# A gated MLP behind a softmax convolution on one core: the transposes one step later, the exponentials two steps earlier, and the carried tokens loaded in eight pieces

## The chip, the core and the metric

The kernel runs on one NeuronCore of a Trainium2 chip. TensorE (PE, with its weight loads shown apart as PEld) multiplies, VectorE (DVE), ScalarE (ACT) and GpSimd (POOL) work on the elements, and SyncE (SP) issues every DMA. The metric is the device time of one execution in microseconds (us). Before the change it is 1408.44 us, the median of three runs from 1408.35 to 1408.87 us.

## What is computed

The reference has two stages. The first is a causal convolution over seven tokens whose weights are a softmax of the input `weight_gen`, one set for each token and head. The second is a gated MLP with 192 inputs, 1536 hidden columns and 192 outputs over all 16384 tokens.

```
w   = exp(weight_gen - max);  w = w / (sum(w) + 1e-9)        # 8 heads, 7 taps
xa[s, h, :] = sum over k of w[s, h, k] * x_pad[s + k, h, :]  # 6 zero rows ahead of each batch
g   = xa @ w_gate                                            # [16384, 1536]
out = (g * sigmoid(g) * (xa @ w_val)) @ w_out                # [16384, 192]
```

The weights of the MLP come as 64-bit floats; the convolution's inputs are 32-bit.

## The kernel before

**Tiles.** Each of the 128 partitions holds 128 consecutive tokens, and a batch of 4096 tokens fills 32 partitions. The work goes over 32 *groups* of 4 tokens per partition, that is 512 tokens each. A group has 12 *steps*, one for each block of 128 hidden columns, so there are 384 steps, and step `i` is block `f = i % 12` of group `g = i // 12`.

**One step on TensorE.** `up_first` (L439, L442) and `up_second` (L451) multiply the transposed activations by the step's columns of both weight matrices, in three products of rounded and remainder parts each, into two PSUM buffers. ACT makes `sg`, the silu of the first buffer (L459); DVE makes `h`, the product with the second buffer (L473), and with that both buffers are read; ACT rounds it to `hi` (L474) and DVE takes the remainder `lo` (L476). Two to three steps later (`LAG = 2`) `down` (L503, L512; L496 in group 0) multiplies `hi` and `lo` by the output weights. The pool `ps_up` has four buffers, so a step's two are asked for again two steps later.

**Getting the next group ready.** During group `g - 1`, DVE makes the convolution of group `g`: seven products (L230) and their sums into `xatt` (L260), spread over nine steps. The last sum is followed by a copy on ACT (L263) that fills the second half of `xatt`. Then PE transposes `xatt` in two halves (`turn`, L299) into two more buffers of `ps_up` (tile `tr`), and ACT and DVE split the result into `xhi` (L317) and `xlo` (L324). In the step that transposes, the transposes stand on PE's queue right behind `up_first`, and the downs that a step normally has between `up_first` and `up_second` come after `up_second`. With `s0 = 12 (g - 1) - 3` (for group 1 it is -1), the sums are spread over the steps from `s0` to `s0 + 8`, and the table `turned` puts the transposes into step `s0 + 9`; that is block `f = 6` of the group before, with the last sum in block `f = 5`.

**The softmax.** The taps come in six chunks. For a chunk, DVE takes maxima and differences (L169, L176), ACT one exponential over the whole chunk (L182, 128x1344), DVE sums, reciprocals and products (L187 to L199). The exponential needs another function table than silu: ACT loads a table ahead of it and another behind it, ahead of the next silu. The table `exps` says in which step it is recorded, between `up_first` and the step's silu. Chunk 1 is recorded in step 16 (`EXP1`), and chunks 2 to 5 in steps 66, 138, 210 and 282, each time block `f = 6`.

**The head.** Ahead of step 0, SP issues the first taps, the first `x` (L141), the *carried tokens* and then the raw MLP weights (L348). The carried tokens are the last six of the partition before, which the convolution of a partition's first tokens needs; each batch's first partition has zeros instead (L149). `load_x` fetches them in four loads of 31 partitions (L150). DVE and POOL then make group 0's convolution and turn the 64-bit weights into 32-bit ones (`weight_ops`, L362 to L402), block by block, four raw blocks ahead. In group 0 DVE does all of a step's other work ahead of the step's `h` (here written as `hi`, L468).

The order on every engine is the order in which the code records the work. `spread` gives each small operation a step; within a step, the first goes between `h` and `lo`, the others behind.

Of the kernel before, what the change touches and what calls it, by code (L numbers as in the profile page):

```python
# [18 lines left out]
def dynconv_glu_kernel(  # L19
# [23 lines left out]
    nc = tc.nc  # L43
# [4 lines left out]
    P = 128  # L48
    T = B * S // P
    PAD = K - 1  # L50
# [4 lines left out]
    NF = F // P  # L55
# [4 lines left out]
    EXP1 = 16  # L60
# [34 lines left out]
    xr = x.rearrange("b (q t) d -> (b q) t d", t=T)  # L95
# [24 lines left out]
    def load_taps(c):  # L120

        j0, n = wcuts[c]
        wt = w_t[c] = soft.tile([P, NJ, H, K], F32, tag="wt", name="wt")
        pieces = {0: (0, JG, n), 1: range(0, n + 1, 2 * JG)}.get(c, (0, n))

        def load(a, b):
            nc.sync.dma_start(
                out=wt[:, a:b].rearrange("p t h k -> p t (h k)"), in_=wgr[:, j0 + a : j0 + b]
            )

        return [lambda a=a, b=b: load(a, b) for a, b in zip(pieces, pieces[1:])]

    def load_x(c):

        j0, n = xcuts[c]
        xt = x_t[c] = xin.tile([P, PAD + NX, D], F32, tag="xt", name="xt")
        pieces = {0: (0, JG, n), 1: range(0, n + 1, 2)}.get(c, (0, n))

        def load(a, b):
            own = PAD if c and a == 0 else 0  # L140
            nc.sync.dma_start(  # L141
                out=xt[:, PAD + a - own : PAD + b], in_=xr[:, j0 + a - own : j0 + b]
            )
            if c == 0 and a == 0:


                per = S // T
                for p0 in range(0, P, per):
                    nc.gpsimd.memset(xt[p0 : p0 + 1, 0:PAD], 0.0)  # L149
                    nc.sync.dma_start(  # L150
                        out=xt[p0 + 1 : p0 + per, 0:PAD],
                        in_=xr[p0 : p0 + per - 1, T - PAD : T],
                    )

        return [lambda a=a, b=b: load(a, b) for a, b in zip(pieces, pieces[1:])]

# [387 lines left out]
    turned = {}  # L544

    def spread(ops, first, last):

        for n, op in enumerate(ops):
            at = first + (n * (last - first)) // len(ops)
            todo.setdefault(max(at, 0), []).append(op)  # L550

    with tc.manual_schedule():
# [44 lines left out]
        for c in range(1, len(wcuts)):  # L597
            s0 = (wcuts[c - 1][0] // JG - 1) * NF - LEAD if c > 1 else NF
            s1 = (wcuts[c][0] // JG - 1) * NF - LEAD
            before, exponentials, after = softmax_ops(c)  # L600
            at = s0 + (s1 - s0) * 5 // 8 if c > 1 else EXP1
            if c + 1 < len(wcuts):
                todo.setdefault(s1, []).append(lambda c=c: load_taps(c + 1)[0]())
            spread(before, s0 + 1 - (c == 1), at)
            exps[at] = exponentials
            spread(after, at + 2, s1)
        for g in range(1, NG):
            s0 = (g - 1) * NF - (LEAD if g > 1 else LEAD1)
            c = first_x.get(g)
            if c and c + 1 < len(xcuts):  # L610
                todo.setdefault(s0, []).append(lambda c=c: load_x(c + 1)[0]())
            asides, rest, _ = attention_ops(g)
            spread(asides, max(s0, 0), s0 + NF - 4)
            spread(rest, max(s0, 0), s0 + NF - 3)
            turned[s0 + NF - 3] = g

        steps = [(g, f) for g in range(NG) for f in range(NF)]
        for i in range(len(steps) + LAG + 1):
            ops = todo.pop(i, [])
            to_turn = turned.get(i)  # L620
            if i < len(steps):
                g, f = steps[i]
# [75 lines left out]
```

## Time and profile before

| | before |
|---|---|
| median of the runs | 1408.44 us |
| the profiled execution | 1409.2 us, of which 1407.4 us are the span from the first to the last instruction |
| PE busy | 1300.9 us, 92% of the span |
| DVE, ACT, POOL busy | 1010.4 us, 610.2 us, 71.8 us |
| granted TensorE clock, mean | 0.988 |
| chain that ended last, by engine | PE 83%, DVE 8%, ACT 4%, DMA 2% |

The profile is of one execution. A bracket behind a row of the timeline says how long the engine sat idle before the instruction and which event ended that; the chain of waits is followed back from the last instruction. A `q` behind an engine's name means its sequencer.

### The profile page before, as it was taken

Reading aid. Unit: us, or ns where it says so; the run is one execution under the profiler, and the core shown is the slowest. Engines: PE = TensorE matmul, PEld = TensorE weight load, DVE = VectorE, ACT = ScalarE, POOL = GpSimd, SP = SyncE. Lnnn points to the kernel's source line nnn. Section 1 sums busy time; section 2 is a strip of 40 time slices with the busy share of each in tenths; the row PEclk is TensorE's granted clock in tenths of the full one; section 3 lists DMA queues with packets and bytes.
Section 4 is the critical chain, followed back from the end, with each engine's and each line's share of the span. In section 5 each row is a group of like instructions: output and inputs, shape, how many; then the busy total and the mean of one; then the engine's idle time right before and its main releaser. Section 6 shows DMA issues by size and latency. Waiting matters only on the chain.

```text
span 1407.4 us, 31625 instructions
## 1 busy us (share of the span) xinstructions
PE 1300.9 (92%) x13560; PEld 1220.4 (87%) x13560; DVE 1010.4 (72%) x1385; ACT 610.2 (43%) x1073; POOL 71.8 (5%) x66
## 2 busy tenths in 40 slices
PE   0479999999999999999999999999999999999998
PEld 0359899989999998999999899989989899999998
DVE  2997867768777777877777777777777776677743
ACT  1445444454444445444344544444454444444443
POOL 3673000000000000000000000000000000000000
PEclk9989999999999999999999999999999999999999
DMA  3341010101001010100101001010100101000000
GB/s 96 97 156 32 13 41 13 52 13 51 13 21 52 13 52 12 51 13 21 52 13 52 13 22 43 18 51 13 52 13 13 41 13 52 13 13 13 13 13 13
DMA packets 28460, 47.36 MB, mean 34 GB/s; under 512 B 1956, under 2 KB 25508, under 8 KB 26528
## 3 DMA queue, kind: packets, MB, share of 16 engines
q1 hardware_dynamic: 28320, 45.34, 9.7%
q8 instruction: 106, 1.74, 0.5%
q14 instruction: 34, 0.28, 0.1%
HBM read 32.75 MB, written 12.58 MB: 32 GB/s over the span
## 4 chain that ended last, share of the span: by engine, by line
PE 83%; DVE 8%; ACT 4%; DMA 2%; issue 1%; SPq 0%; ACTq 0%; DVEq 0%
PE dn L503 22%; PE up L451 19%; PE up L439 18%; PE up L442 17%; PE dn L512 6%; DVE xatt L260 3%; DVE h L473 2%; DMA xt<-in_x_dram 2%; ACT sg L459 2%; PE tr L299 1%; ACT xatt L263 1%; DVE m L389 1%; DVE w L402 1%; DVE m L379 0%; PE dn L496 0%
## 5 line engine op out<-in xcount | busy, mean ns | idle before, releaser
L503 PE MATMUL dn<-wo,hi 64*128 64x384 f32 x2976 | 612.7, 347 | 0.4 <-ACT hi L474 0.4
L512 PE MATMUL dn<-wo,lo 64*128 64x192 f32 x2976 | 543.0, 249 | 0.3 <-DVE lo L476 0.3
L503 PEld LDWEIGHTS dn<-wo,hi 64*128 64x128 f32 x2976 | 480.0, 185 | 14.9 <-ACT hi L474 0.6
L473 DVE TENSOR_TENSOR h<-up,sg 128x512 f32<-128x512 f32 x372 | 257.1, 691 | 289.5 <-ACT sg L459 289.4
L512 PEld LDWEIGHTS dn<-wo,lo 64*128 64x128 f32 x2976 | 444.8, 187 | 9.6 <-DVE lo L476 0.5
L459 ACT ACTIVATE sg<-up 128x512 f32<-128x512 f32 x384 | 229.7, 598 | 435.7 <-PE up L451 405.0
L474 ACT ACTIVATE hi<-h 128x512 fp32r<-128x512 f32 x372 | 235.2, 632 | 294.7 <-DVE h L473 294.7
L476 DVE TENSOR_TENSOR lo<-h,hi 128x512 fp32r<-128x512 f32 x372 | 255.8, 688 | 70.5 <-ACT hi L474 70.5
L439 PE MATMUL up<-xhi,wb_hi 64*128 64x512 f32 x768 | 246.8, 425 | 10.8 <-ACT sg L459 7.5
L451 PE MATMUL up<-xhi,wa_hi 64*128 64x512 f32 x768 | 240.4, 427 | 9.8 <-POOLq L280 9.7
L439 PE MATMUL up<-xlo,wb_hi 64*128 64x512 f32 x768 | 234.0, 395 | 0.9 <-DVE xlo L324 0.9
L439 PE MATMUL up<-xhi,wb_lo 64*128 64x512 f32 x768 | 234.0, 396 | 0.0
L442 PE MATMUL up<-xhi,wa_lo 64*128 64x512 f32 x768 | 233.0, 393 | 0.0
L442 PE MATMUL up<-xhi,wa_hi 64*128 64x512 f32 x768 | 233.0, 393 | 0.0
L442 PE MATMUL up<-xlo,wa_hi 64*128 64x512 f32 x768 | 231.8, 390 | 0.0
L451 PE MATMUL up<-xhi,wa_lo 64*128 64x512 f32 x768 | 226.1, 392 | 0.0
L451 PE MATMUL up<-xlo,wa_hi 64*128 64x512 f32 x768 | 225.6, 391 | 0.0
L230 DVE TENSOR_TENSOR prod<-xt,wt 128x768 f32<-128x768 f32 x186 | 182.0, 979 | 0.1
L260 DVE TENSOR_TENSOR xatt<-xatt,prod 128x768 f32<-128x768 f32 x186 | 180.7, 971 | 0.0
L439 PEld LDWEIGHTS up<-xhi,wb_hi 64*128 64x128 f32 x768 | 138.3, 186 | 16.4 <-ACT sg L459 8.3
L442 PEld LDWEIGHTS up<-xlo,wa_hi 64*128 64x128 f32 x768 | 138.9, 187 | 8.1
L442 PEld LDWEIGHTS up<-xhi,wa_lo 64*128 64x128 f32 x768 | 138.1, 185 | 8.8
(57 smaller groups left out, 1370.3 us busy)
## 6 DMA issues: line engine op xcount, KB each, us to landing
xt<-in_x_dram SPq DMA_DIRECT2D x14, 1344.0 KB, 5.6
out_dram<-osb SPq DMA_DIRECT2D x31, 384.0 KB, 2.6
raw<-in_moe_w_out_dram SPq DMA_DIRECT2D x12, 192.0 KB, 2.7
wt<-in_weight_gen_dram SPq DMA_DIRECT2D x3, 672.0 KB, 3.9
raw<-in_moe_w_gate_dram SPq DMA_DIRECT2D x12, 128.0 KB, 2.6
raw<-in_moe_w_val_dram SPq DMA_DIRECT2D x12, 128.0 KB, 2.6
wt<-in_weight_gen_dram SPq DMA_DIRECT2D x4, 224.0 KB, 3.7
xt<-in_x_dram SPq DMA_DIRECT2D x2, 384.0 KB, 3.7
```

Of the source, the lines that this page charges most:

```text
L230: engine.tensor_tensor(out=into.rearrange("p t (h i) -> p t h i", h=H), in0=src, in1=w, op=ALU.mult)
L260: nc.vector.tensor_tensor(out=a, in0=a, in1=tmp.pop(k), op=ALU.add)
L263: nc.scalar.activation(out=a[:, :, D:], in_=a[:, :, P:D], func=AF.Copy)
L439: nc.tensor.matmul(ps, w[r, fs], m[r], start=(n == 0), stop=False)
L442: ins = nc.tensor.matmul(sums[i], w[r, i, fs], m[r], start=False, stop=False)
L451: ins = nc.tensor.matmul(sums[i], w[r, i, fs], m[r], start=False, stop=(n == len(full) - 1))
L459: nc.scalar.activation(out=sg, in_=sums[0], func=AF.Silu)
L473: nc.vector.tensor_tensor(out=h, in0=sums[1], in1=sg, op=ALU.mult)
L474: nc.scalar.activation(out=hi, in_=h, func=AF.Copy)
L476: nc.vector.tensor_tensor(out=lo, in0=h, in1=hi.bitcast(F32), op=ALU.subtract)
L503: nc.tensor.matmul(acc[t], hi[r, cs], wo[r, f].rearrange("p a d -> p (a d)"), start=opens, stop=False,)
L512: nc.tensor.matmul(acc[t][:, 0:D], lo[r, cs], wo[r, f, 0], start=False, stop=closes)
```

## The change

Three things change in the code. `load_x` zeroes the four rows first and then issues eight loads in place of four, 15 and 16 partitions each; what is loaded is the same, and so is the queue. The exponentials of chunks 2 to 5 are recorded two steps earlier (64, 136, 208 and 280, block `f = 4`), and with them the maxima and differences ahead of them are spread over two steps fewer, the sums behind them over two steps more; chunk 1 stays in step 16. The transposes of every group are recorded one step later (`s0 + 10`, block `f = 7`; for group 1 step 9 in place of 8), while the sums that they read stay where they are.

```diff
                 for p0 in range(0, P, per):
                     nc.gpsimd.memset(xt[p0 : p0 + 1, 0:PAD], 0.0)
-                    nc.sync.dma_start(
-                        out=xt[p0 + 1 : p0 + per, 0:PAD],
-                        in_=xr[p0 : p0 + per - 1, T - PAD : T],
-                    )
+                for p0 in range(0, P, per):
+                    for q0, q1 in ((p0 + 1, p0 + per // 2), (p0 + per // 2, p0 + per)):
+                        nc.sync.dma_start(
+                            out=xt[q0:q1, 0:PAD], in_=xr[q0 - 1 : q1 - 1, T - PAD : T]
+                        )
...
-            at = s0 + (s1 - s0) * 5 // 8 if c > 1 else EXP1
+            at = s0 + (s1 - s0) * 5 // 8 - 2 if c > 1 else EXP1
...
-            turned[s0 + NF - 3] = g
+            turned[s0 + NF - 2] = g
```

From the middle of the program on, the changed kernel's line numbers are one higher (L460 is the silu that was L459).

SP's queue at the head of the program, before: the taps, the first `x`, the carried tokens, the first raw weights.

```order
L127 DMA wt<-in_weight_gen_dram 128x448
L141 DMA xt<-in_x_dram 128x768
L150 DMA xt<-in_x_dram 31x1152 x4
L348 DMA raw<-in_moe_w_gate_dram 128x256
L348 DMA raw<-in_moe_w_val_dram 128x256
```

And with the change:

```order
L127 DMA wt<-in_weight_gen_dram 128x448
L141 DMA xt<-in_x_dram 128x768
L152 DMA xt<-in_x_dram 15x1152
L152 DMA xt<-in_x_dram 16x1152
L152 DMA xt<-in_x_dram 15x1152
L152 DMA xt<-in_x_dram 16x1152
L152 DMA xt<-in_x_dram 15x1152
L152 DMA xt<-in_x_dram 16x1152
L152 DMA xt<-in_x_dram 15x1152
L152 DMA xt<-in_x_dram 16x1152
L349 DMA raw<-in_moe_w_gate_dram 128x256
```

The raw weights stand behind eight loads now, four before.

DVE's queue in group 5, from the `h` of block `f = 4` on, before. The second `xatt` row is the last sum of group 6, and `xlo` reads what PE transposed.

```order
L473 TENSOR_TENSOR h<-up,sg 128x512
L260 TENSOR_TENSOR xatt<-xatt,prod 128x4x192
L476 TENSOR_TENSOR lo<-h,hi 128x512
L473 TENSOR_TENSOR h<-up,sg 128x512
L260 TENSOR_TENSOR xatt<-xatt,prod 128x4x192
L476 TENSOR_TENSOR lo<-h,hi 128x512
L473 TENSOR_TENSOR h<-up,sg 128x512
L476 TENSOR_TENSOR lo<-h,hi 128x512
L324 TENSOR_TENSOR xlo<-tr,xhi 128x512 x2
```

The same place with the change:

```order
L474 TENSOR_TENSOR h<-up,sg 128x512
L261 TENSOR_TENSOR xatt<-xatt,prod 128x4x192
L477 TENSOR_TENSOR lo<-h,hi 128x512
L474 TENSOR_TENSOR h<-up,sg 128x512
L261 TENSOR_TENSOR xatt<-xatt,prod 128x4x192
L477 TENSOR_TENSOR lo<-h,hi 128x512
L474 TENSOR_TENSOR h<-up,sg 128x512
L188 TENSOR_REDUCE sm<-wt 128x96
L477 TENSOR_TENSOR lo<-h,hi 128x512
L474 TENSOR_TENSOR h<-up,sg 128x512
L477 TENSOR_TENSOR lo<-h,hi 128x512
L325 TENSOR_TENSOR xlo<-tr,xhi 128x512 x2
```

Two `h` and two `lo` stand between the last sum and `xlo`, one of each before; the chunk's first sum (`sm`) has come into block `f = 6`.

ACT's queue in group 5, from the silu of block `f = 5` on, before:

```order
L459 ACTIVATE sg<-up 128x512
L474 ACTIVATE hi<-h 128x512
L263 ACTIVATE xatt<-xatt 128x4x64
L182 ACT_TABLE_LOAD
L182 ACTIVATE wt<-wt 128x1344
L459 ACT_TABLE_LOAD
L459 ACTIVATE sg<-up 128x512
L474 ACTIVATE hi<-h 128x512
L317 ACTIVATE xhi<-tr 128x512 x2
```

And with the change, from the exponential on:

```order
L183 ACT_TABLE_LOAD
L183 ACTIVATE wt<-wt 128x1344
L460 ACT_TABLE_LOAD
L460 ACTIVATE sg<-up 128x512
L475 ACTIVATE hi<-h 128x512
L460 ACTIVATE sg<-up 128x512
L475 ACTIVATE hi<-h 128x512
L264 ACTIVATE xatt<-xatt 128x4x64
```

The exponential with its two table loads stands ahead of the silu of block `f = 4`, and two silus come before the copy into `xatt`; it stood right behind that copy, ahead of the silu of the block that transposes.

## Rows read from the trace of the kernel before

**Rows 1.** The page's head: the span, and the first engines' busy time, share of the span and instructions.

```profile
span 1407.4 us, 31625 instructions
PE 1300.9 (92%) x13560; PEld 1220.4 (87%) x13560; DVE 1010.4 (72%) x1385; ACT 610.2 (43%) x1073; POOL 71.8 (5%) x66
```

**Rows 2.** The timeline of the first 60 us: start, length, engine, line, operation, tiles, shape, count, and in brackets the idle time before it and what ended it.

```profile
2.12 6.03 SPq L150 DMA_DIRECT2D xt<-in_x_dram  x4
...
6.18 0.39 DVE L199 TENSOR_TENSOR wt<-wt,sm 128x224 f32<-128x224 f32 x1
...
28.99 0.96 DVE L230 TENSOR_TENSOR xatt<-xt,wt 128x768 f32<-128x768 f32 x1 [22.42 <-DMA xt<-in_x_dram]
...
29.40 0.60 SPq L348 DMA_DIRECT2D raw<-in_moe_w_val_dram  x1
...
36.52 0.45 DVE L362 TENSOR_SCALAR e<-raw 128x576 int32<-128x576 int32 x1
...
47.82 1.97 PE L292 MATMUL tr<-ident,xatt 128*128 128x128 f32 x8 [47.82 <-DVE xatt L260]
```

**Rows 3.** The chain of waits in the first 130 us: start, length, what it went through.

```profile
2.80 0.31 SPq L150
...
3.16 25.71 DMA xt<-in_x_dram
...
103.55 0.61 DVE hi L468
...
104.30 0.66 PE tr L299 x7
```

**Rows 4.** The DMA engines in the first 35 us: the rate in 40 slices of 0.875 us, and two groups of issues with their count, size and time from issue to landing.

```profile
GB/s 0 0 201 280 351 11 11 26 26 26 26 26 26 26 26 26 160 100 94 93 30 111 299 75 26 26 26 47 141 26 26 26 25 23 94 120 293 329 317 212
...
xt<-in_x_dram SPq DMA_DIRECT2D x4, 139.5 KB
...
wt<-in_weight_gen_dram SPq DMA_DIRECT2D x1, 224.0 KB, 2.6
```

**Rows 5.** Busy time by stretch, from 7 to 14 us: the last three numbers are the granted PE clock, the mean busy share of the 16 DMA engines, and GB/s.

```profile
7.00:14.00 7.00, 0.00 (x0) 0.00 (x0) 0.00 (x0) 0.32 (x2) 0.00 (x0) 1.00 0.06 26
```

**Rows 6.** The timeline of ACT, cut to the silu of block `f = 0` in four groups: 5, 6, 24 and 31.

```profile
287.75 0.60 ACT L459 ACTIVATE sg<-up 128x512 f32<-128x512 f32 x1 [1.22 <-PE up L451]
...
332.72 0.60 ACT L459 ACTIVATE sg<-up 128x512 f32<-128x512 f32 x1 [1.22 <-PE up L451]
...
1077.53 0.60 ACT L459 ACTIVATE sg<-up 128x512 f32<-128x512 f32 x1 [1.23 <-PE up L451]
...
1363.01 0.60 ACT L459 ACTIVATE sg<-up 128x512 f32<-128x512 f32 x1 [1.22 <-PE up L451]
```

**Rows 7.** The timeline of PE and its weight loads in group 10, around the step that transposes: the first matmul of three steps in a row (508.51, 511.71, 517.03), the end of `up_first` and the transposes.

```profile
508.51 0.41 PE L439 MATMUL up<-xhi,wb_hi 64*128 64x512 f32 x1
...
511.71 0.41 PE L439 MATMUL up<-xhi,wb_hi 64*128 64x512 f32 x1
...
512.88 0.58 PE L442 MATMUL up<-xhi,wa_lo 64*128 64x512 f32 x2
...
514.23 0.76 PE L299 MATMUL tr<-ident,xatt 64*128 64x64 f32 x7 [0.76 <-DVE xatt L260]
...
514.59 0.27 PEld L299 LDWEIGHTS tr<-ident,xatt 64*128 64x128 f32 x6 [0.25 <-ACT xatt L263]
...
517.03 0.74 PE L439 MATMUL up<-xhi,wb_hi 64*128 64x512 f32 x2
```

**Rows 8.** The chain of waits at the same place.

```profile
511.89 0.61 ACT sg L459
...
512.53 0.69 DVE h L473
513.22 0.87 DVE xatt L260
...
514.12 0.43 ACT xatt L263
```

**Rows 9.** Who waited for whom over the whole span: microseconds in all, times, the longest.

```profile
PE tr L299 <- DVE xatt L260: 27.7, 31, 4.3
```

**Rows 10.** Group 5 behind the exponential: PE's timeline at the next step's first matmul, and the busy times and the granted clock (third number from the end) of a stretch behind it.

```profile
311.04 0.50 PE L439 MATMUL up<-xhi,wb_hi 64*128 64x512 f32 x1 [1.91 <-ACT sg L459]
...
313.00:316.50 3.50, 3.50 (x25) 3.33 (x24) 1.30 (x3) 0.35 (x1) 0.00 (x0) 0.51 0.02 5
```

**Rows 11.** The timeline of PE in group 1, steps 17 and 18, behind the exponential of chunk 1 in step 16: the first matmul of three steps (135.80, 139.24, 145.80), and the transposes.

```profile
135.80 0.41 PE L439 MATMUL up<-xhi,wb_hi 64*128 64x512 f32 x2
...
139.24 0.50 PE L439 MATMUL up<-xhi,wb_hi 64*128 64x512 f32 x1
139.96 0.49 PE L439 MATMUL up<-xhi,wb_hi 64*128 64x512 f32 x1 [0.23 <-DVE h L473]
...
142.99 0.76 PE L299 MATMUL tr<-ident,xatt 64*128 64x64 f32 x7 [1.37 <-DVE xatt L260]
...
145.80 0.73 PE L439 MATMUL up<-xhi,wb_hi 64*128 64x512 f32 x2
```

**Rows 12.** Busy time by stretch: group 10 with its transposes, and a stretch of group 31, which has none; the third number from the end is the granted PE clock.

```profile
495.87:536.60 40.73, 39.85 (x427) 37.81 (x425) 29.73 (x42) 17.68 (x31) 0.00 (x0) 1.00 0.13 45
...
1346.00:1390.00 44.00, 44.00 (x467) 42.67 (x465) 19.70 (x29) 18.11 (x31) 0.00 (x0) 1.00 0.04 11
```

**Rows 13.** The timeline of PE in group 0, step 8, which transposes for group 1.

```profile
103.70 0.34 PE L299 MATMUL tr<-ident,xatt 64*128 64x64 f32 x1 [4.30 <-DVE xatt L260]
```

## The prediction

> **What bounds the kernel now.** I read the page's head first: PE is busy for 92% of the span [rows 1], so the kernel is TensorE's, and what can be won is where PE waits. The timeline of the head shows the largest place: PE does nothing before 47.82 us [rows 2]. Then the list of waits shows one that comes back in every group: PE's transposes wait for DVE's last sum, 31 times, 27.7 us in all [rows 9]. Last, the spacing of the groups shows a third. From group 24 to group 31, seven groups take 1363.01 - 1077.53 = 285.48 us, 40.78 each; group 5 alone takes 332.72 - 287.75 = 44.97 [rows 6]. The change touches each of the three places with one edit.
>
> **The carried tokens.** DVE has its first softmax weights ready at 6.18 + 0.39 = 6.57 us and then stands idle for 22.42 us until the loads from `x` have landed, at 28.99 [rows 2]; the chain has 25.71 us of load there [rows 3]. Four loads of 139.5 KB are 571 KB, and through this stretch the rate is 26 GB/s [rows 4], which makes 22 us. The DMA engines' mean busy share is 0.06 [rows 5], one engine in sixteen: the four loads of 31 partitions run on a single engine, while 201 to 351 GB/s flowed for the loads of 128 partitions just before [rows 4]. The Trainium skill gives a rule for this, in DMA: Bandwidth & Descriptors, section "Why a DMA increments its semaphore by 16 and not by 1": a copy is spread over the largest number of engines up to 16 that divides its outer size. By it 31 goes to one engine, as the trace shows, 15 to fifteen and 16 to sixteen; no row here has a load of 15 or 16.
>
> When do eight loads land? Issuing starts at 2.12 [rows 2]. The quickest issue of these loads took from 2.80 to 3.16, 0.36 with the gap [rows 3]; the slow kind among the raw weights takes 0.60 [rows 2], about 0.64 with a like gap. The eighth is so issued between 2.12 + 7 x 0.36 = 4.6 and 2.12 + 7 x 0.64 = 6.6, and a load of 224 KB landed 2.6 us after its issue [rows 4]. That gives 7.2 to 9.2, and no earlier than 6.57, when DVE is ready. I take 8.0, the middle, because the loads of 128 partitions move at about 280 GB/s until 4.4 us and 571 KB more at that rate end at 6.4, ahead of their landing. **Gain 28.99 - 8.0 = 21.0 us, between 19.8 and 22.4.**
>
> What is late next? DVE needs the first raw weights 36.52 - 28.99 = 7.5 us behind its start, so at 15.5. Their five loads stand behind the eight on SP's queue: issued by 5.9 + 5 x 0.64 = 9.1 at the slow pace, landed 2.6 later at 11.7. The four blocks loaded ahead had queued up behind the carried tokens before; now they flow. DVE's chain then moves as a whole, with PE behind it: up to 104.30 the chain goes from DVE to PE [rows 3].
>
> **The transposes.** In a usual group `up_first` of the transposing step ends at 512.88 + 0.58 = 513.46, and the transposes begin at 514.23: 0.76 of waiting, and 0.25 more before the second half's weight load, which needs ACT's copy [rows 7]. The chain shows why: silu 511.89, `h` 512.53, the last sum 513.22, the copy 514.12, ending at 514.55 [rows 8]. With the transposes a step later (517.03 - 511.71 = 5.32 for the transposing step, 511.71 - 508.51 = 3.20 for another [rows 7]) the sums have 3.20 us more, against 1.0 us of waiting, so the wait goes. The transposes also need the two buffers that `h` of the step before frees; `h` ends at 512.53 + 0.69 = 513.22, 0.24 before `up_first` does, and this order stays the same a step later. Gain 1.0 each, 0.76 if the second wait stays. Of the 31 transposing steps, those for groups 1 and 2 are apart; the 29 for groups 3 to 31 give **29 x 1.0 = 29.0 us, between 22.0 and 32.** The splits of `xhi` and `xlo` move too; they end some three steps before group `g` begins, and blocks `f = 6` to `8` have no sums for DVE.
>
> Group 2's transposes, in step 18, wait 1.37 [rows 11], behind a late `h`: gain 1.6 with the 0.25. Group 1's wait 4.30 in step 8 [rows 13], but there DVE is the bound: its `h` of step 7 ends at 103.55 + 0.61 = 104.16 [rows 3], and PE resumes then whatever it has next. It gains only what it can do of step 8 within the wait, and waits for the next `h` instead: I take 0.5, between -1.5 and 4.3.
>
> **The exponentials.** Groups 5 to 23, 19 of them, hold chunks 2 to 5: 1077.53 - 287.75 = 789.78, against 19 x 40.78 = 774.82 [rows 6]. The four cost 15.0 us over the usual, 3.7 each. In group 5 the next step's first matmul waits 1.91 for the late silu, and behind that wait the granted clock is 0.51 over 313.0 to 316.5 [rows 10], the lower of the two levels. The place is bad because the transposes hold two of the four buffers: the next step asks for the very buffers that the late silu and `h` are to free, instead of having a step's grace.
>
> What do they cost at `f = 4`? Chunk 1 stands there already (16 = 12 + 4). The step after it takes 139.24 - 135.80 = 3.44 against 3.20, and the one after that, which transposes, 145.80 - 139.24 = 6.56 against 5.32 [rows 7, 11]; of that 1.24, 1.37 - 0.76 = 0.61 is a longer wait for the sum, counted above. Left are 0.24 + 0.63 = 0.87. **Gain 15.0 - 4 x 0.87 = 11.5 us**, 8.6 if each costs 1.6, 14.2 if each costs 0.2. Three steps lie now between exponential and transposes, two around chunk 1 before.
>
> **Sum.** 21.0 + 29.0 + 1.6 + 0.5 + 11.5 = 63.6. The profiled execution took 1409.2 us, 0.8 over the median, and should come to 1345.6; 1408.44 - 63.6 = 1344.8 for the median: **1345 us**. With the bounds of the terms taken together, but not all at one end, 1339 to 1353.
>
> **Rivals.**
>
> *The exponentials stall PE at `f = 4` as well.* DVE has sums to make in blocks 4 and 5 and none in 6, so it could catch up more slowly. Against it stands chunk 1, at the same `f` and with more DVE work around it, with a wait of 0.23 [rows 11]. If all 15.0 stay: 1344.8 + 11.5 = 1356. Chance 0.10.
>
> *The wait of the transposes stays, on other buffers.* If PE waits for `h` to free the buffers, not for the sum, moving by a step gives nothing. `h` ends 0.24 before `up_first` [rows 7, 8], which is little. 1344.8 + 29.0 = 1374. Chance 0.05.
>
> *Loads of 15 partitions stay on one engine.* Four of 69 KB, 276 KB at 26 GB/s [rows 4], are 10.6 us; with the slow start before 6.1 us they land near 18: 10 us back, 1355. Chance 0.05.
>
> *Slower: the clock.* Group 5 takes 44.97 - 40.78 = 4.19 us over the usual [rows 6]; 1.91 of it is the wait, and the other 2.28 lie in the stretch at 0.51 behind it [rows 10]. If PE fell to the lower level for such a stretch once at each of the 35 places (31 transposes, 4 exponentials), the price is 35 x 2.28 = 80 us and the time 1425. It decides from 28 places on (63.6 / 2.28). Against it: the transposes cost no clock where they stand now, 1.00 over group 10, and 1.00 over 44 us without any wait [rows 12]. The Trainium skill speaks for it in TensorE: Matmul & The Clock Gate, section "Part 4: PE-mode transpose": a transpose does not count as PE being busy as a matmul does. Group 10 shows that eight and eight of them among matmuls do not matter here. Chance 0.02.
>
> **How the numbers follow.** All three edits work about as sized: 0.76. The three milder rivals have 0.20, the slower one 0.02, and 0.02 stay for what I have not seen. The range should hold 8 in 10: my case nearly whole and the rivals near 1355, 1339 to 1357. The runs of before differ by 0.04%, so a change of 0.2%, 2.8 us, can be told from none. All but the last rival lie far below 1405: faster 0.97, same 0.01, slower 0.02.
>
> **What would show it.** The first L231 on DVE should start near 8 us, and PE's first matmul near 26.8. The list of waits should have no line of the transposes for the last sum of more than a microsecond or two outside group 0. The groups should be spaced 39.8 us, those with an exponential at most 1 us more, with the clock at 1.00 in them. I am wrong if the transposes wait for `h` or for DVE's `lo` instead, if a group with an exponential still takes 4 us more, or if DVE, early, waits for raw weights in the first 50 us.

## The result, and the profile after

The changed kernel takes 1341.12 us, the median of four runs from 1340.54 to 1342.55, against 1408.65 us for the kernel before on the same chip: a ratio of 0.9522, with a 95% interval from 0.9505 to 0.9538. The forecast was 1345, with a range of 1339 to 1357. The profiled execution took 1342.55 us and its span fell from 1407.4 to 1340.8, by 66.6 us, where the prediction's terms sum to 63.6.

The page's head, to be read beside [rows 1]:

```profile
span 1340.8 us, 31630 instructions
PE 1287.4 (96%) x13560; PEld 1205.6 (90%) x13560; DVE 1010.5 (75%) x1385; ACT 608.5 (45%) x1073; POOL 71.8 (5%) x66
```

The instructions are the old ones but for a few, and DVE's and ACT's busy times are the same to 2 us. PE's busy time fell by 13.5 us, for the same 13560 matmuls; the other 53.1 us that went are PE's waiting. PE's share of the span is 96% now.

**The head.** The timeline of the first 30 us, as in [rows 2]:

```profile
2.12 4.97 SPq L152 DMA_DIRECT2D xt<-in_x_dram  x8
...
9.32 2.29 DVE L231 TENSOR_TENSOR xatt<-xt,wt 128x768 f32<-128x768 f32 x1 [2.22 <-DMA raw<-in_moe_w_gate_dram]
...
28.12 1.97 PE L293 MATMUL tr<-ident,xatt 128*128 128x128 f32 x8 [28.12 <-DVE xatt L261]
```

DVE waits 2.22 us where it waited 22.42, and PE's first matmul comes at 28.12 instead of 47.82: 19.7 us. (The bracket names the transfer that landed at the same time by the profile; the product reads `x`, and the last carried load lands at 8.95.) The busy times from 5.0 to 6.5 us, to be held against [rows 5], and SP's own waits in the first 60 us:

```profile
5.00:6.50 1.50, 0.00 (x0) 0.00 (x0) 1.40 (x5) 0.68 (x2) 0.79 (x3) 1.00 0.90 166
```

```profile
SPq L152 <- DMA xt<-in_x_dram: 1.5, 1, 1.5
```

In this stretch every packet of more than 4 bytes has 4608 bytes, one row of a carried load, and the DMA share is 0.90 in place of 0.06: loads of 15 and 16 partitions use nearly all engines. SP held the eighth load back for 1.5 us. That wait is the program's own: in SP's order of instructions a load waits for the semaphore of the one eight places ahead of it. Here that is the load of `x` issued at 1.65, and by the chain of the head it landed 5.11 later, at 6.76.

**The groups.** The timeline of ACT, cut to the silu of block `f = 0` in groups 4, 5, 6, 24 and 31, as in [rows 6]:

```profile
219.39 0.60 ACT L460 ACTIVATE sg<-up 128x512 f32<-128x512 f32 x1 [1.23 <-PE up L452]
...
259.56 0.60 ACT L460 ACTIVATE sg<-up 128x512 f32<-128x512 f32 x1 [0.71 <-PE up L452]
...
300.07 0.60 ACT L460 ACTIVATE sg<-up 128x512 f32<-128x512 f32 x1 [1.22 <-PE up L452]
...
1016.33 0.60 ACT L460 ACTIVATE sg<-up 128x512 f32<-128x512 f32 x1 [1.23 <-PE up L452]
...
1293.16 0.60 ACT L460 ACTIVATE sg<-up 128x512 f32<-128x512 f32 x1 [1.23 <-PE up L452]
```

Groups 24 to 30 take (1293.16 - 1016.33) / 7 = 39.55 us each, where they took 40.78. Group 5, with an exponential, takes 300.07 - 259.56 = 40.51 instead of 44.97. But group 4, with no exponential at all, takes 259.56 - 219.39 = 40.17: 0.62 more than its like.

**The transposes.** The timeline of PE in group 6, as in [rows 7]: the step's first matmul, the end of `up_first`, the transposes, the next step's first matmul. Behind it the waits that the transposes have over the whole span, in place of [rows 9]:

```profile
322.38 0.41 PE L440 MATMUL up<-xhi,wb_hi 64*128 64x512 f32 x1
...
323.56 0.56 PE L443 MATMUL up<-xhi,wa_lo 64*128 64x512 f32 x2
323.79 0.58 PE L300 MATMUL tr<-ident,xatt 64*128 64x64 f32 x8
...
326.45 0.71 PE L440 MATMUL up<-xhi,wb_hi 64*128 64x512 f32 x2
```

```profile
PEld tr L300 <- DVE h L474: 8.0, 30, 0.6
...
PE tr L300 <- DVE h L474: 1.8, 4, 0.5
```

The transposing step takes 326.45 - 322.38 = 4.07 us instead of 5.32. No line is left in which these transposes wait for the last sum. In its place stands `h`, which frees their two buffers: 30 small waits of the weight loads, and 4 of PE proper. These four are the groups ahead of an exponential, and here is the first of them, in group 4 (DVE, then ACT, then PE, from three timelines):

```profile
239.89 0.85 DVE L177 TENSOR_TENSOR wt<-wt,mx 128x672 f32<-128x672 f32 x1
240.67 0.69 DVE L477 TENSOR_TENSOR lo<-h,hi 128x512 fp32r<-128x512 f32 x1
241.28 0.95 DVE L261 TENSOR_TENSOR xatt<-xatt,prod 128x768 f32<-128x768 f32 x1
243.21 0.69 DVE L474 TENSOR_TENSOR h<-up,sg 128x512 f32<-128x512 f32 x1 [0.97 <-ACT sg L460]
...
242.27 0.42 ACT L264 ACTIVATE xatt<-xatt 128x256 f32<-128x256 f32 x1 [1.63 <-DVE xatt L261]
242.59 0.58 ACT L460 ACTIVATE sg<-up 128x512 f32<-128x512 f32 x1
...
243.95 0.40 PE L300 MATMUL tr<-ident,xatt 64*128 64x64 f32 x6 [0.46 <-DVE h L474]
```

Read it in order: the chunk's last difference (L177) stands in block `f = 5` ahead of the group's last sum, because the differences were spread over two steps fewer. The sum goes behind `lo` and starts at 241.28, 1.39 later than the place right behind `h` that it has elsewhere (239.89). ACT's copy of the sum waits for it (1.63), and the silu of the next step stands behind that copy on ACT's queue. So `h` is late, and with it the buffers for the transposes. Before the change the same difference stood in block `f = 7` (step 55), behind the last sum and the transposes.

**The exponential.** ACT's timeline in group 5, and PE's wait in the step behind it, beside [rows 10]:

```profile
274.41 1.28 ACT L183 ACT_TABLE_LOAD   x1
275.70 1.33 ACT L183 ACTIVATE wt<-wt 128x1344 f32<-128x1344 f32 x1
277.05 1.28 ACT L460 ACT_TABLE_LOAD   x1
278.34 0.60 ACT L460 ACTIVATE sg<-up 128x512 f32<-128x512 f32 x1
...
279.72 0.50 PE L440 MATMUL up<-xhi,wb_hi 64*128 64x512 f32 x1 [0.23 <-DVE h L474]
```

The two table loads and the exponential still hold ACT for 3.9 us ahead of the silu, but PE waits only 0.23 in the next step, not 1.91. The busy times of group 5 have the granted clock at 1.00 (third number from the end) over the whole group, where the stretch behind the wait in [rows 10] had 0.51:

```profile
259.00:299.50 40.50, 40.27 (x428) 36.92 (x426) 30.11 (x44) 21.41 (x34) 0.00 (x0) 1.00 0.04 11
```

### The profile page after: what moved, and what is told of

It reads as the page before. It is cut to its first block, busy times and chain, and to the rows that moved or that the text cites. A ratio compares the mean times of both kernels' runs of the same rounds, so it can differ in the third digit from the quotient of the medians.

```text
span 1340.8 us, 31630 instructions
## 1 busy us (share of the span) xinstructions
PE 1287.4 (96%) x13560; PEld 1205.6 (90%) x13560; DVE 1010.5 (75%) x1385; ACT 608.5 (45%) x1073; POOL 71.8 (5%) x66
## 4 chain that ended last, share of the span: by engine, by line
PE 88%; DVE 5%; ACT 3%; DMA 2%; issue 1%; SPq 1%; POOL 0%; ACTq 0%; DVEq 0%; POOLq 0%
PE dn L504 22%; PE up L440 21%; PE up L452 20%; PE up L443 18%; PE dn L513 5%; PE tr L300 1%; DVE h L474 1%; DMA xt<-in_x_dram 1%; SPq L349 1%; ACT sg L460 1%; DVE xatt L261 1%; DMA raw<-in_moe_w_gate_dram 1%; DVE m L390 1%; ACT wt L183 0%; ACT L460 0%
## 5 line engine op out<-in xcount | busy, mean ns | idle before, releaser
L504 PE MATMUL dn<-wo,hi 64*128 64x384 f32 x2976 | 599.6, 346 | 0.4 <-ACT hi L475 0.4
L513 PE MATMUL dn<-wo,lo 64*128 64x192 f32 x2976 | 531.7, 248 | 0.3 <-DVE lo L477 0.3
L460 ACT ACTIVATE sg<-up 128x512 f32<-128x512 f32 x384 | 229.4, 597 | 381.3 <-PE up L452 347.0
L440 PE MATMUL up<-xhi,wb_hi 64*128 64x512 f32 x768 | 242.4, 424 | 5.3 <-DVE hi L469 3.4
L452 PE MATMUL up<-xhi,wa_hi 64*128 64x512 f32 x768 | 234.2, 426 | 11.5 <-POOLq L281 11.4
L440 PE MATMUL up<-xlo,wb_hi 64*128 64x512 f32 x768 | 229.2, 394 | 0.9 <-DVE xlo L325 0.9
L440 PE MATMUL up<-xhi,wb_lo 64*128 64x512 f32 x768 | 229.0, 395 | 0.0
L443 PE MATMUL up<-xhi,wa_hi 64*128 64x512 f32 x768 | 227.6, 392 | 0.0
L443 PE MATMUL up<-xhi,wa_lo 64*128 64x512 f32 x768 | 227.6, 392 | 0.0
L443 PE MATMUL up<-xlo,wa_hi 64*128 64x512 f32 x768 | 226.7, 390 | 0.0
L452 PE MATMUL up<-xhi,wa_lo 64*128 64x512 f32 x768 | 220.3, 392 | 0.0
L452 PE MATMUL up<-xlo,wa_hi 64*128 64x512 f32 x768 | 219.5, 390 | 0.0
L443 PEld LDWEIGHTS up<-xhi,wa_hi 64*128 64x128 f32 x768 | 137.0, 186 | 9.3
```

The lines of the kernel that those rows point to most:

```text
L440: nc.tensor.matmul(ps, w[r, fs], m[r], start=(n == 0), stop=False)
L443: ins = nc.tensor.matmul(sums[i], w[r, i, fs], m[r], start=False, stop=False)
L452: ins = nc.tensor.matmul(sums[i], w[r, i, fs], m[r], start=False, stop=(n == len(full) - 1))
L460: nc.scalar.activation(out=sg, in_=sums[0], func=AF.Silu)
L504: nc.tensor.matmul(acc[t], hi[r, cs], wo[r, f].rearrange("p a d -> p (a d)"), start=opens, stop=False,)
L513: nc.tensor.matmul(acc[t][:, 0:D], lo[r, cs], wo[r, f, 0], start=False, stop=closes)
```

## The experiments

**Each part alone.** The three parts were made one at a time, on the kernel before. A group's time here and below is counted, as in [rows 6], from its silu of block `f = 0` to the next group's.

The loads alone:

```diff
-                    nc.sync.dma_start(
-                        out=xt[p0 + 1 : p0 + per, 0:PAD],
-                        in_=xr[p0 : p0 + per - 1, T - PAD : T],
-                    )
+                for p0 in range(0, P, per):
+                    for q0, q1 in ((p0 + 1, p0 + per // 2), (p0 + per // 2, p0 + per)):
...
```

> Only the carried tokens' eight loads; exponentials and transposes as before. Theory: the head moves as a whole, by what PE's first matmul moved in the changed kernel, 47.82 - 28.1 = 19.7 us, and nothing behind it: 1408.65 - 19.7 = 1389.0 us, groups still 40.78 apart. Rival: the head's gain is partly eaten by DVE and PE waits in group 0 that the put-off transposes relieved; then it is under 18 us, over 1390.6.

Measured: 1390.91 us, ratio 0.9865 (0.9851 to 0.9878); its span is 17.9 us below that of before. DVE and PE start as early as in the changed kernel, and the usual groups stay at 40.78. The rival's size came, in another place: of the head's gain 1.3 us is lost in step 18, group 2's transposes behind the exponential of chunk 1, which takes 7.88 us instead of 6.56 [rows 11]. The transposes wait there about as long as before, 1.40 us in place of 1.37, but behind the wait the granted clock is 0.74 over 125 to 129 us. With the transposes put off, in e2 and in the changed kernel, that loss is gone.

The transposes alone:

```diff
-            turned[s0 + NF - 3] = g
+            turned[s0 + NF - 2] = g
```

> Only the transposes one step later; the exponentials stay in steps 66, 138, 210 and 282, one step ahead of the transposes. Theory: each group's 1.25 us go (29 of them), and 2 us in groups 0 and 1, 38 in all; but an exponential one step ahead of the transposes still delays the h whose buffers the transposes take, so its four places stay near 15 us: 1370.5 us. Rival: it is enough that exponential and transposes are not in one step; then the four cost 4 us in all and the time is about 1359.5.

Measured: 1373.06 us, ratio 0.9736 (0.9723 to 0.9749). Usual groups take 39.55 us: the move alone is worth the whole 1.2 us per group. The groups with an exponential take 44.09, 42.85, 44.08 and 43.89 (groups 5, 11, 17, 23; group 11 alone shows no lower clock). PE's timeline in group 5 shows what took the place of the old wait, and the busy times behind it what followed:

```profile
306.37 0.27 PE L299 MATMUL tr<-ident,xatt 64*128 64x64 f32 x1 [2.44 <-ACT sg L459]
307.10 0.40 PE L299 MATMUL tr<-ident,xatt 64*128 64x64 f32 x6 [0.45 <-DVE h L473]
```

```profile
307.00:312.00 5.00, 4.90 (x45) 4.89 (x47) 2.66 (x5) 2.95 (x5) 0.00 (x0) 0.66 0.01 3
```

Without the third part the exponential stands one step ahead of the transposes, and these wait 2.44 + 0.45 for the buffers that the late silu and `h` free; then the clock falls, 0.66 over the next 5 us.

The exponentials alone:

```diff
-            at = s0 + (s1 - s0) * 5 // 8 if c > 1 else EXP1
+            at = s0 + (s1 - s0) * 5 // 8 - 2 if c > 1 else EXP1
```

> Only the exponentials two steps earlier, with the maxima and differences spread over two steps fewer; the transposes stay in block f = 6, two steps behind the exponential. Theory: a place costs what chunk 1 costs in the kernel before, 1.5 us, in place of 3.7, which gives 9 us back; but the last difference now stands ahead of the last sum in groups 4, 10, 16 and 22, where the transposes wait for that sum in the next step: 1.5 us more each, 6 in all. So 1405.6 us. Rival: the moved difference costs nothing there, and the time is 1399.6.

Measured: 1411.53 us, ratio 1.0014 (1.0005 to 1.0023): a miss, it gains nothing and costs about 2 us. The groups with an exponential do fall, to 42.34, 42.36, 43.57 and 43.37 (groups 5, 11, 17 and 23), but groups 4, 10, 16 and 22 ahead of them rise to 43.40, 43.42, 42.17 and 42.17. DVE's and PE's timelines in group 4:

```profile
265.97 0.85 DVE L176 TENSOR_TENSOR wt<-wt,mx 128x672 f32<-128x672 f32 x1
...
267.36 0.95 DVE L260 TENSOR_TENSOR xatt<-xatt,prod 128x768 f32<-128x768 f32 x1
...
268.46 0.76 PE L299 MATMUL tr<-ident,xatt 64*128 64x64 f32 x7 [2.15 <-DVE xatt L260]
```

The difference stands ahead of the last sum here as well, and the transposes, one step behind that sum, pay for it at once: 2.15 where the usual wait is 0.76 [rows 7]. The clock is 0.72 over 268.5 to 272 us; in group 16 it is 1.00 behind the same wait of 2.15, which is the 1.2 us between the two groups. So the third part gains nothing without the second: the medians change by -18.5, -36.4 and +2.1 us for the three alone, -52.7 in sum; the changed kernel's by -67.5.

**The difference one step later.** What group 4 showed in the changed kernel is tried by moving the last difference from step 53 to 54, behind the last sum:

```diff
-            spread(before, s0 + 1 - (c == 1), at)
+            spread(before, s0 + 1 - (c == 1), at + (c > 1))
```

> The changed kernel with the last difference of chunks 2 to 5 one step later (block f = 6 in place of f = 5, groups 4, 10, 16, 22), nothing else. Theory: in these groups the difference pushed the last sum, ACT's copy of it stood ahead of the next silu and delayed that, and the transposes then waited 0.46 for h; with it gone the groups come from 40.15 to 39.53, 4 x 0.62 = 2.5 us: 1338.6 us. Rival: the 0.6 us are the cost of the difference itself on a full DVE, wherever it stands: no change, 1341.1.

Measured: 1339.11 us, ratio 0.9496 (0.9483 to 0.9509). The silu of block `f = 0` in groups 4, 5 and 6:

```profile
218.47 0.60 ACT L460 ACTIVATE sg<-up 128x512 f32<-128x512 f32 x1 [1.23 <-PE up L452]
...
258.04 0.60 ACT L460 ACTIVATE sg<-up 128x512 f32<-128x512 f32 x1 [0.71 <-PE up L452]
...
298.51 0.60 ACT L460 ACTIVATE sg<-up 128x512 f32<-128x512 f32 x1 [1.22 <-PE up L452]
```

Group 4 is back at 258.04 - 218.47 = 39.57 us, and group 5 stays at 40.47. The wait ahead of the exponential was the difference, as the timelines said: four times 0.62 = 2.5 us by the groups, 2.0 by the medians.

**Loads of 17 and 14 partitions.** The changed kernel with the same bytes in as many loads, cut elsewhere:

```diff
-                    for q0, q1 in ((p0 + 1, p0 + per // 2), (p0 + per // 2, p0 + per)):
+                    for q0, q1 in ((p0 + 1, p0 + 18), (p0 + 18, p0 + per)):
```

> The changed kernel with the eight loads cut into 17 and 14 partitions in place of 15 and 16: as many loads, as many bytes, the same queue. Theory (the number of engines goes by the divisors of the number of partitions): 17 partitions run on one engine, four of them are 313 KB, at 26 GB/s 12.0 us; DVE then starts its first product near 18 us in place of 9.32, and the time is 8 to 9 us over the changed kernel's, about 1350 us (ratio to before 0.958). Rival (smaller loads land sooner because eight are in flight in place of four): DVE starts at 9 to 10 us and the time stays at 1341 us, ratio 0.952.

Measured: 1353.42 us, ratio 0.9602 (0.9588 to 0.9617). The rates of the first 35 us in 40 slices, and DVE's first product:

```profile
GB/s 0 0 186 268 351 156 91 26 95 21 26 26 194 135 26 26 97 91 26 47 286 87 23 56 196 115 274 301 354 230 290 204 183 155 0 0 0 0 203 170
```

```profile
20.34 2.28 DVE L231 TENSOR_TENSOR xatt<-xt,wt 128x768 f32<-128x768 f32 x1 [13.34 <-DMA raw<-in_moe_w_gate_dram]
```

The 26 GB/s of [rows 4] are back between the bursts of the other loads, and DVE starts 11.0 us later than with 15 and 16, at 20.34, over 2 us later than expected. So it is the count of partitions in a load that decides, and not that there are eight of them. The Trainium skill's rule (DMA: Bandwidth & Descriptors, section "Why a DMA increments its semaphore by 16 and not by 1") gives the same: no number up to 16 divides seventeen but 1. The trace agrees with one engine's rate, 26 GB/s. The run also tells about what the prediction's rival "loads of 15 partitions stay on one engine" would have cost: 12.3 us with loads of 17, where it was put at 10 with loads of 15.

**The own tokens' load between the carried ones.** In the changed kernel SP held a carried load until a load of `x` had landed. Here that load is issued behind the fourth carried load (on the version of e4):

```diff
...
+            carry(carried[:4])
             nc.sync.dma_start(
                 out=xt[:, PAD + a - own : PAD + b], in_=xr[:, j0 + a - own : j0 + b]
             )
+            carry(carried[4:])
```

> The kernel of e4 with the first load of the own tokens issued behind the fourth of the eight loads in place of ahead of all. Theory (the eighth load was held on SP until 6.78 us, because only eight loads of SP are in flight and it waited for the own tokens' 384 KB): no load waits, the last is issued by 6 us, DVE starts at 8.3 us in place of 9.32, 1 us less in all, 1338 us. Rival (the 1.3 MB at some 250 GB/s set the time, not the issue): DVE starts at 9.3 us or later, no gain.

Measured: 1339.68 us, ratio 0.9509 (0.9493 to 0.9525), no gain over e4. SP's second batch of carried loads and DVE's first product:

```profile
3.90 1.75 SPq L153 DMA_DIRECT2D xt<-in_x_dram  x4
...
9.13 2.28 DVE L238 TENSOR_TENSOR xatt<-xt,wt 128x768 f32<-128x768 f32 x1 [1.85 <-DMA raw<-in_moe_w_val_dram]
```

All loads are issued by 5.65, 1.4 us earlier than in the changed kernel, and DVE still starts at 9.13 instead of 9.32, and later than in e4, at 8.97. The start isn't the same from run to run: with the very loads of the changed kernel it is 8.37 in the profile of e9 (below) and 9.35 in that of e1:

```profile
8.37 2.29 DVE L231 TENSOR_TENSOR xatt<-xt,wt 128x768 f32<-128x768 f32 x1 [1.80 <-DMA raw<-in_moe_w_val_dram]
```

Within this spread the run shows no gain from issuing sooner; a few tenths either way would not be seen.

**The exponential behind its step's silu.** In e4's version the exponential is recorded behind the silu of its step and not ahead of it, so that this step's `h` isn't late:

```diff
-                if i in exps:
-                    exps[i]()
...
                 sg = silu(sums)
+                if i in exps:
+                    exps[i]()
```

> The kernel of e4 with the exponential (all five chunks) recorded right behind the step's silu in place of ahead of it, so that its table load runs while ACT waits for h, and the round part hi stands between the exponential and the second table load. Theory (what is left of an exponential's cost, 0.94 us a chunk, is the silu that comes 2.7 us late against a grace of two steps): the next silu is now about 1.9 us late, its h still ahead of the matmuls that take its buffers, and the cost goes, 4 us in all: 1335 us, ratio 0.947. Rival (ACT's 3.9 us have to be made up by PE wherever they stand, or the downs now wait for the late hi): 1339 us or more, ratio 0.950.

Measured: 1339.37 us, ratio 0.9503 (0.9488 to 0.9517), no gain. Group 5 takes 40.65 us. ACT's and PE's timelines at the transposes, three steps behind the exponential:

```profile
281.42 0.42 ACT L264 ACTIVATE xatt<-xatt 128x256 f32<-128x256 f32 x1 [0.23 <-DVE xatt L261]
...
282.37 0.27 PE L300 MATMUL tr<-ident,xatt 64*128 64x64 f32 x1 [0.18 <-ACT sg L460]
283.10 0.40 PE L300 MATMUL tr<-ident,xatt 64*128 64x64 f32 x6 [0.46 <-DVE h L474]
```

The steps with and right behind the exponential now run at 3.20 to 3.22 us without a wait, but ACT and DVE are still late two steps on, where the sum, its copy and the silu queue up behind each other, and the transposes pay: 0.18 + 0.46 listed, and about 1.1 us in the step, by the group's 40.65. The cost had only moved.

**Two further steps earlier.** Two runs take the exponentials to block `f = 2`, five steps ahead of the transposes, with the differences and sums around them in the steps that they have in e4. In e8 the exponential stands behind the silu of its step, in e9 ahead of it:

```diff
-            at = s0 + (s1 - s0) * 5 // 8 - 2 if c > 1 else EXP1
+            at = s0 + (s1 - s0) * 5 // 8 - 4 if c > 1 else EXP1
...
-            spread(before, s0 + 1 - (c == 1), at + (c > 1))
+            spread(before, s0 + 1 - (c == 1), at + 3 * (c > 1))
...
-            spread(after, at + 2, s1)
+            spread(after, at + 2 + 2 * (c > 1), s1)
```

> The last difference later (as in the run e4) and the exponential behind its step's silu (as in e6), with the exponentials of chunks 2 to 5 two further steps earlier, in block f = 2, five steps ahead of the transposes instead of three; the last difference and the sums behind the exponential stay in the steps that they had in e4. Theory (in e6 the exponential cost nothing in its own step and was paid only because the late copy, silu and h of the second step behind it were still late when the transposes asked for their buffers): ACT and DVE have caught up before the transposes, the groups with an exponential come to 39.55 to 39.75 us against 40.5 in e4 and 40.6 in e6, 1339.1 - 4 x 0.9 = 1335.5 us, ratio 0.947. Rival (a table load and an exponential on ACT cost PE about one microsecond wherever they stand, since ACT's lost 4 us must be made up from h's buffers): groups stay at 40.4 to 40.6, 1339 us, ratio 0.950.

Measured: 1335.38 us (1334.18 to 1336.80), ratio 0.9474 (0.9461 to 0.9487), the fastest kernel of this study. ACT's timeline ahead of the transposes, and the busy times of the 39.5 us around it:

```profile
280.09 0.60 ACT L460 ACTIVATE sg<-up 128x512 f32<-128x512 f32 x1 [0.40 <-PE up L452]
```

```profile
258.50:298.00 39.50, 39.50 (x426) 37.51 (x426) 30.38 (x44) 21.25 (x34) 0.00 (x0) 1.00 0.04 12
```

The silu behind the copy of the last sum waits for PE again (0.40) and not for ACT's queue: ACT has caught up. PE is busy for all of the 39.50 us, and the group takes 39.57. The exponentials now cost nothing that can be seen in a group.

> As e8, but with the exponential ahead of its step's silu, where the change has it: e4 with the exponentials two further steps earlier. It tells apart distance and place. Theory (ahead of the silu, h of the exponential's own step comes late and the next step's up_first or downs wait for it, whatever stands two or five steps on): 40.4 to 40.5 in the groups with an exponential, as in e4, 1339 us, ratio 0.950. Rival (only the distance to the transposes counts): 39.6 to 39.8, 1336 us, ratio 0.947.

Measured: 1348.56 us, ratio 0.9567 (0.9554 to 0.9580): 9.5 us slower than e4, and neither the theory nor the rival. The groups with an exponential take 43.53, 43.73, 42.13 and 43.48. ACT's and PE's timelines in group 5, and the line of the list of waits over the whole span:

```profile
266.31 1.32 ACT L183 ACTIVATE wt<-wt 128x1344 f32<-128x1344 f32 x1
267.54 0.85 ACT L529 ACTIVATE osb<-dn 128x384 f32<-128x384 f32 x2
...
268.07 1.07 PE L504 MATMUL dn<-wo,hi 64*128 64x384 f32 x2 [1.97 <-ACT osb L529]
```

```profile
PE dn L504 <- ACT osb L529: 7.7, 4, 2.0
```

In block `f = 2` ACT also copies the last group's outputs out of `dn` (L529), and the first downs of the new group need those buffers. Ahead of the silu the exponential stands between the two pairs of copies, and PE waits 1.97 us for the second; behind the silu, in e8, all four copies are done before it. So the distance to the transposes counts, but so does what stands behind the exponential on ACT's queue.

## Why the prediction was right, and where its sizes were off

The three mechanisms, their places and their order of size came out as forecast; 1341.1 lies in the likeliest case's own range. That the sum is off by 3 us alone is in part luck: one term is 6.8 us too small, and two together are 3.9 too large. Term by term, in the profiled executions:

| term | forecast | measured |
|---|---|---|
| carried tokens | 21.0 | 19.7 |
| transposes, groups 3 to 31 | 29.0 | 29 x 1.236 = 35.8 |
| transposes, groups 1 and 2 | 0.5 + 1.6 | 0.35 + 1.79 |
| exponentials | 11.5 | 8.9 |
| sum | 63.6 | 66.6 |

**The carried tokens: right, and 1.3 too much.** The step that was off is the start at 8.0 us; DVE started at 9.32, just past the upper of the two bounds (9.2). The eighth load was issued at 6.78, after the hold on SP that the prediction didn't count, and landed at 8.95; the seven ahead of it took 3.5 to 4.9 us to land, not the 2.6 us taken from the load of 224 KB. In e9's profile the same loads let DVE start at 8.37, so up to 1.0 us of the 1.3 is what runs differ by. e7, where the loads were issued sooner, gained nothing by it. The raw weights were in time, as argued: from DVE's first product to PE's first matmul it is 18.80 us, 18.83 before [rows 2].

**The transposes: right, and mis-sized by a fifth.** A term of 1.0 was read from the idle times, 0.76 + 0.25 [rows 7]; each group gained 1.24 (40.78 - 39.55, before rounding 1.236). The idle time in a bracket starts at the modelled end of the last matmul, but matmuls of `up_first` start 0.23 us apart and last longer than that, so that part of a wait lies under the last one. From the last start listed for `up_first` to the transposes it was 514.23 - 512.88 = 1.35, and is 323.79 - 323.56 = 0.23 now: 1.12 us, to which the second half's wait adds the rest. The spacing of steps would have given the size: the transposes need 0.87 us of PE (4.07 - 3.20), while the transposing step took 2.12 more than another before (5.32 - 3.20). The upper bound of 1.1 was too low.

That PE's transposes do not wait for `h` instead was right for 27 groups and wrong for four: the argument that `h` ends 0.24 ahead of `up_first`, "and this order stays the same a step later", missed that in four groups the exponentials' edit moves a difference of 0.85 us ahead of the last sum and thereby delays `h` itself. The margin is as thin as it looked: 30 weight loads still wait for `h`, 8.0 us in all, mostly hidden.

**The exponentials: the price per exponential right, one effect left out.** Each was to cost 0.87 at block `f = 4`; the four groups with one take 0.95 on average in three and 0.74 in the fourth, over 39.55. The step that failed is the same one: the edit was costed at the exponential, and its spread differences were not counted where they landed. So of the 15.0 us there are 3.6 left in the groups with an exponential and 2.5 in groups 4, 10, 16 and 22; e4 gives the 2.5 back. This was in the order of DVE's instructions in block `f = 5` of those groups, and the prediction looked at the group behind.

The prediction also added its terms as if they were independent. They aren't: alone, the exponentials' edit is worth nothing (e3) and that of the transposes leaves their groups at 42.9 to 44.1 us (e2). Its price for an exponential at `f = 4` was read at chunk 1 with the transposes two steps behind, of which 0.61 was counted with the sum's wait, that is 1.48 in all. With two steps, in e3, groups 5 and 11 do take 1.6 over 40.78, and the other two 2.8 and 2.6; the changed kernel has three steps, for which no row before had a price. That about 0.87 came out there, 0.9 on average, is in part luck.

The slower clock was over-priced. The prediction gave the wait 1.91 and the clock behind it 2.28 of group 5's 4.19 us. Group 11 of the same profile has the same wait, with the clock at 1.00 behind it: ACT's silus of block `f = 0` in groups 11 and 12, PE's wait, and the busy times behind it:

```profile
536.60 0.60 ACT L459 ACTIVATE sg<-up 128x512 f32<-128x512 f32 x1 [1.23 <-PE up L451]
...
579.98 0.60 ACT L459 ACTIVATE sg<-up 128x512 f32<-128x512 f32 x1 [1.22 <-PE up L451]
...
559.87 0.50 PE L439 MATMUL up<-xhi,wb_hi 64*128 64x512 f32 x1 [1.91 <-ACT sg L459]
...
562.00:565.50 3.50, 3.50 (x41) 3.23 (x39) 1.82 (x3) 1.01 (x3) 0.00 (x0) 1.00 0.02 5
```

That group takes 579.98 - 536.60 = 43.38 us, 2.6 over the usual, so the lower clock cost group 5 1.6 us and not 2.28. At that price all 35 places would have cost 56 us, less than the 63.6 of the forecast gain.

**The rivals.** None of the milder three came, but the second is there in small: 0.46 us in four groups. e5 shows the third was real as a mechanism, for loads of 17. The slower one, the clock falling at 35 places, did not come: from 91.2 us to the last 4 us of the span the clock is 1.00. But its mechanism is there: the clock falls behind a wait of 2.89 in e2 (0.66) and of 2.15 in e3 (0.72), as behind 1.91 in [rows 10]. In the changed kernel the longest wait at one of the 35 places is 0.46 us, and none outside group 0 shows a lower clock.

What stays open: PE's waits in groups 0 and 1 and the clock there differ between runs, and group 0 takes 63.9 to 66.3 us in these profiles (the clock is 0.62 over 84 to 93 us in the changed kernel's); which instruction decides that was not tried. Nor does any run show why the clock falls behind one stall and not behind its like.

## What to carry to other kernels

When an operation is moved past others on an in-order engine, list everything that moves with it, small feeders as well, and look at each place where a piece lands: 0.85 us of DVE ahead of the wrong sum cost 2.5 us in all, and the same exponential cost nothing, 1 or 4 us by its distance to the transposes and by what stood behind it on ACT's queue. Read the size of a wait from the spacing of steps with and without it, not from the idle time in brackets. Edits that share buffers are worth trying together before one of them is dropped: the exponentials' edit alone gained nothing, and it was part of a change worth 67.5 us where the three alone sum to 52.7.

## What was not expected of the hardware

A stall of PE can cost clock on top of the waiting, and the same stall does not always do so. Groups 5 and 11 of the kernel before, 1.6 us apart, are one such pair, groups 4 and 16 of e3, 1.2 apart, another. In e9 the wait behind ACT's copy was 1.97 us in group 5 and again in group 17; the busy times of the 5 us behind each have the granted clock third from the end:

```profile
268.00:273.00 5.00, 4.93 (x35) 4.84 (x37) 3.12 (x4) 2.90 (x5) 0.00 (x0) 0.66 0.25 79
...
751.00:756.00 5.00, 5.00 (x51) 4.95 (x52) 3.87 (x6) 3.14 (x5) 0.00 (x0) 1.00 0.24 79
```

Group 5 took 43.53 us, 4.0 over the usual; group 17, where the clock stayed at its upper level of 2.4 GHz, took 42.13, 2.6 over. So the clock cost 1.4 us there, less than the wait. A difference of a microsecond or two between two kernels can be no more than that: from group 1 to group 30, e3's profile shows the lower clock in groups 1, 4, 10, 17 and 23, that of before in 5, 17 and 23, and e3 is 2.1 us slower.
